# One PSUM tile for two columns, replaced after the first stage by a tile for each column

## The chip, the cores and the metric

The kernel runs on one core of a Trainium2 chip. The metric is the device time of one execution in microseconds. The median of three runs is 1278.3 us (1278.21 to 1280.56). Every duration below comes from one profiled execution.

## The reference

A channel attention is followed by two feed-forward layers, all in float32, for 6016 tokens of 256 channels.

```python
s = kn.transpose(0, 2, 1) @ qn / tau       # 256 x 256, norms over the tokens
a = softmax(s);  x = (v @ a)               # 6016 x 256
h = x @ w_in                               # 256 -> 2048
P = a0 + a1*h + a2*h**2 + a3*h**3
Q = 1 + |b0|*|h| + |b1|*h**2
y = (P / (Q + 1e-6)) @ w_out               # 2048 -> 256
gate = 1 / (1 + exp(-(y @ w_gate)))        # 256 -> 1536
val = y @ w_val
out = (gate * val) @ w_out2                # 1536 -> 256
```

## The kernel before

**Stages.** A first stage loads q and k, forms the 256 x 256 scores and the norms, and folds the attention matrix into w_in. It also converts the weights, and each float32 weight and activation becomes a high and a low part in float32r. From then on the tokens go through in 12 blocks: one of 384 tokens and eleven of 512. A block passes `moe1` (eight steps j of two 128-row slices of the 2048 hidden rows) and then `moe2` (twelve steps f of 128 rows of the 1536). `moe2` of a block is interleaved with `moe1` of the next, and the last block's `moe2` runs alone at the end, called the tail below.

**One step of `moe1`.** TensorE (PE) writes twelve matmuls of 512 columns into the two-bank tile `pH` (L796, L798, L800). ScalarE (ACT) reads `pH` three times (L808, L810, L806). VectorE (DVE) forms the fraction with L818, L812, L826, L815, L830 and L833. The last reader of `pH` is L815, called "the w product" below, and only then can the next step's matmuls write `pH`, which has one buffer. ACT rounds the result (L836), GpSimd (POOL) subtracts for the low part (L841), and PE multiplies with w_out into `pY` (L849, L851, L859).

**One step f of `moe2`.** Six matmuls form the gate column G(f) and six more the value column V(f), both 128 x 512, by the same lines L894, L896 and L898. The name of the weight (`wg` or `wv`) tells them apart. ACT takes the sigmoid of G(f) (L907, called sig(f)), DVE multiplies it with V(f) (L909, called sv(f)), ACT rounds (L912), POOL subtracts (L916), and PE multiplies with w_out2 into `pO` (L923, L931). When L870 and L872 have read `pY` of a block, the results are `yhi` and `ylo`, which G and V read.

**Where G and V lie.** PSUM has eight banks. `pH`, `pY` and `pO` take two each. The last two are the tile `gv` of shape [128, 2, 512], allocated once for the whole kernel. The class `Half` hands out `gv[:, 0, :]` for the tag `pG` and `gv[:, 1, :]` for `pV`, a bank each. The first stage and `moe1` of the first block also use both halves together (weight conversion, norms, and the temporary of four of the eight steps of the first block).

**What sets the order.** The class `Plan` holds every operation with a cost and a due time, simulates the five engines, and emits the operations in the order of the simulated starts. In its rules G(f+1) follows sig(f), V(f+1) follows sv(f), and the two columns have nothing to do with each other. The Tile framework then turns accesses to tiles into semaphore waits, in the order of emission. Each engine runs its own instructions in that order.

Of the kernel before, what the change touches and what calls it, by code (L numbers as in the profile page):

```python
# [9 lines left out]
F32 = mybir.dt.float32  # L10
# [5 lines left out]
PSUM = bass.MemoryType.PSUM  # L16
# [230 lines left out]
def c_act(n, psum, aps=0):  # L247
    return (0.052 + 0.000832 * n if psum else 0.093 + 0.000834 * n) + 0.093 * aps


def c_dve(n, aps=0):
    return 0.069 + 0.001041 * n + 0.061 * aps


def c_pool(n):
    return 0.147 + 0.002105 * n


def c_pe(n, passes=1):
    return n / 2400.0 + 0.0133 if passes == 1 else 4 * n / 2400.0 + 0.006  # L260
# [3 lines left out]
def tile_channel_attention_two_moes(  # L264
# [15 lines left out]
    P = 128  # L280
# [5 lines left out]
    NB = 512  # L286
# [20 lines left out]
    wres = ctx.enter_context(tc.tile_pool(name="wres", bufs=1))  # L307
    depth = dict(DEPTH)
    pools = {}
    gv_pool = ctx.enter_context(tc.tile_pool(name="r_gv", bufs=1, space=PSUM))  # L310
    gv = gv_pool.tile([P, 2, NB], F32, name="gv")

    class Half:

        def __init__(self, i):
            self.i = i

        def tile(self, shape, dtype, tag=None, name=None):
            return gv[:, self.i, :]

    for tag, n in depth.items():
        if tag in ("pG", "pV"):
            pools[tag] = Half("GV".index(tag[1]))
            continue
        kw = {"space": PSUM} if tag[0] == "p" else {}
        pools[tag] = ctx.enter_context(tc.tile_pool(name="r_" + tag, bufs=n, **kw))

    ident = const.tile([P, P], F32, name="ident")
    ones = const.tile([P, P], F32, name="ones")
# [547 lines left out]
    def moe2(b_, yhi, ylo):  # L877
        vp = VT if b_ else VT1
        t0, nt = blocks[b_]
        n = nt * P  # L880
        sl_ = slot[min(b_ + 1, NBLK - 1)]
        base = start[b_ + 1] + vp['base'] * sl_ / 8 + WT.get('m%d' % b_, 0.0)
        o_ps = pl.buf("pO", [P, 2, 512], at=start[b_ + 1])
        step = sl_ * NP / F2
        for f in range(F2):
            vt, d = base + f * step, sl_ / 8
            at = start[b_ + 1] + f * step
            gp = [pl.buf("pG", [P, 512], at=at), pl.buf("pV", [P, 512], at=at)]
            sg = pl.buf("sig", [P, NB], at=at)
            hi, lo = (pl.buf(t_, [P, NB], F32R, at=at) for t_ in ("hi2", "lo2"))  # L890
            for i, wt in enumerate((WG, WV)):
                def g_mm(i=i, wt=wt, gp=gp, f=f):
                    for z in range(2):
                        mm(out=gp[i].ap()[:, :n], lhsT=wt.at(f * P, 0, z), rhs=yhi.ap()[:, z, :n],  # L894
                           start=(z == 0), stop=False)
                        mm(out=gp[i].ap()[:, :n], lhsT=wt.at(f * P, 0, z), rhs=ylo.ap()[:, z, :n],  # L896
                           start=False, stop=False)
                        mm(out=gp[i].ap()[:, :n], lhsT=wt.at(f * P, 1, z), rhs=yhi.ap()[:, z, :n],  # L898
                           start=False, stop=(z == 1))
                pl.op(PE, 6 * c_pe(n), vt + (vp['G'] + i * .1) * d, g_mm, [yhi, ylo, wt.key(f * P)], [gp[i]])  # L900

            cuts = [(0, n)] if (b_, f) != (NBLK - 1, F2 - 1) else [(0, n // 2), (n // 2, n - n // 2)]
            wk = WO2.key(f * C)
            for q, (c0, m) in enumerate(cuts):
                sl = slice(c0, c0 + m)
                whole = len(cuts) == 1
                pl.op(ACT, c_act(m, 1), vt + vp['sig'] * d, lambda sg=sg, gp=gp, sl=sl: nc.scalar.activation(  # L907
                    out=sg.ap()[:, sl], in_=gp[0].ap()[:, sl], func=ACTF.Sigmoid), [gp[0]], [(sg, q)])
                pl.op(DVE, c_dve(m), vt + vp['sv'] * d, lambda sg=sg, gp=gp, sl=sl: nc.vector.tensor_tensor(  # L909
                    out=sg.ap()[:, sl], in0=sg.ap()[:, sl], in1=gp[1].ap()[:, sl], op=ALU.mult),  # L910
                    [gp[1], (sg, q)], [(sg, q)])
                pl.op(ACT, c_act(m, 0), vt + vp['hi2'] * d, lambda sg=sg, hi=hi, sl=sl: nc.scalar.activation(  # L912
                    out=hi.ap()[:, sl], in_=sg.ap()[:, sl], func=ACTF.Copy), [(sg, q)], [(hi, q)])
                e = nc.gpsimd if whole else nc.vector
                pl.op(POOL if whole else DVE, c_pool(m) if whole else c_dve(m), vt + vp['lo2'] * d,
                      lambda sg=sg, hi=hi, lo=lo, sl=sl, e=e: e.tensor_tensor(  # L916
                          out=lo.ap()[:, sl], in0=sg.ap()[:, sl], in1=hi.ap()[:, sl].bitcast(F32),
                          op=ALU.subtract), [(sg, q), (hi, q)], [(lo, q)], port=True)

                def o_hi(f=f, hi=hi, sl=sl):  # L920
                    for z in range(2):
                        for i in range(2):
                            mm(out=o_ps.ap()[:, z, sl], lhsT=WO2.at(f * C, i)[:, z * P:(z + 1) * P],  # L923
                               rhs=hi.ap()[:, sl], start=(f == 0 and i == 0), stop=False)

                pl.op(PE, 4 * c_pe(m), vt + vp['oh'] * d, o_hi, [(hi, q), wk], [(o_ps, 0), (o_ps, 1)])
            for zs in ((0, 1),) if whole else ((0,), (1,)):
                def o_lo(f=f, lo=lo, zs=zs, cuts=cuts):
                    for z in zs:
                        for q, (c0, m) in enumerate(cuts):  # L930
                            mm(out=o_ps.ap()[:, z, c0:c0 + m], lhsT=WO2.at(f * C, 0)[:, z * P:(z + 1) * P],  # L931
                               rhs=lo.ap()[:, c0:c0 + m], start=False, stop=(f == F2 - 1 and q == len(cuts) - 1))

                pl.op(PE, len(zs) * sum(c_pe(m) for _, m in cuts), vt + vp['ol'] * d, o_lo,
                      [(lo, q) for q in range(len(cuts))] + [wk], [(o_ps, z) for z in zs])
        ob = pl.buf("v", [P, 2, NB], at=start[b_ + 1] + 1.0)
        vt = base + F2 * step
        if b_ < NBLK - 1:
            pl.op(ACT, c_act(2 * n, 1), vt, lambda: nc.scalar.activation(
                out=ob.ap()[:, :, :n], in_=o_ps.ap()[:, :, :n], func=ACTF.Copy), [(o_ps, 0), (o_ps, 1)], [ob])  # L940
            pl.op(SP, max(.6, nt * .36), vt, lambda: nc.sync.dma_start(
                out=ov[:, :, t0 * P:t0 * P + n], in_=ob.ap()[:, :, :n]), [ob], (), tail=2.0)
        if b_ == NBLK - 1:
            ob2 = pl.buf("v", [P, 2, NB], at=start[b_ + 1] + 1.1)
            pl.op(DVE, c_dve(n), vt, lambda: nc.vector.tensor_copy(
                ob2.ap()[:, 1, :n], o_ps.ap()[:, 1, :n]), [(o_ps, 1)], [ob2])
            pl.op(SP, max(.6, nt * .18), vt, lambda: nc.sync.dma_start(
                out=ov[:, 1, t0 * P:t0 * P + n], in_=ob2.ap()[:, 1, :n]), [ob2], (), tail=2.0)
            pl.op(ACT, c_act(n, 1), vt, lambda: nc.scalar.activation(
                out=ob.ap()[:, 0, :n], in_=o_ps.ap()[:, 0, :n], func=ACTF.Copy), [(o_ps, 0)], [ob])  # L950
            pl.op(ACT, .6, vt, lambda: nc.scalar.dma_start(
                out=ov[:, 0, t0 * P:t0 * P + n], in_=ob.ap()[:, 0, :n]), [ob], (), tail=2.0)
# [49 lines left out]
```

## Time and profile before

| | before |
|---|---|
| median of three runs | 1278.3 us |
| profiled execution, time and span | 1278.6 us, 1276.8 us |
| PE busy | 1199.1 us (94%), 5188 matmuls |
| DVE busy | 985.8 us (77%) |
| ACT busy | 849.5 us (67%) |
| POOL busy | 513.6 us (40%) |
| chain that ended last | PE 71%, DVE 15%, ACT 7%, DMA 5%, issue 2% |

Read the table with two cautions. Matmuls are pipelined, and the modelled length of one (0.39 us) is longer than the distance between two starts. A busy PE therefore says little about time lost on it, which is read from the starts. An engine's idle time matters only where the engine that sets the end waits for it. In the timelines a bracket gives the idle time of the engine before the instruction and what ended it. "PEld" is the loading of weights, which runs one matmul ahead of PE.

### The profile page before, as it was taken

The page shows a single profiled execution, that of the slowest core. Times are in us where ns is not written, and L with a number is a line of the kernel's source. Part 1 is how long each engine was busy: PE and PEld are TensorE (multiplying, and loading weights), DVE is VectorE, ACT ScalarE, POOL GpSimd, SP SyncE. Part 2 cuts the span into 40 slices and gives each one's busy share as a digit, 9 for nine tenths or more (in the row PEclk, how much of TensorE's full clock was granted, in tenths as well). Part 3 has the DMA queues.
Part 4 walks back from the last instruction along what each step waited for, and adds up shares of the span by engine and source line. Part 5 has one row for each costly group of instructions (what it writes and reads, how often), then busy time and mean ns, then how long its engine had stood idle before and what let it go on. Part 6 is the DMA issues. An engine that isn't in the chain of part 4 may idle for free.

```text
span 1276.8 us, 13165 instructions
## 1 busy us (share of the span) xinstructions
PE 1199.1 (94%) x5188; PEld 964.0 (76%) x5188; DVE 985.8 (77%) x844; ACT 849.5 (67%) x996; POOL 513.6 (40%) x262
## 2 busy tenths in 40 slices
PE   7877799999999999999999999999999999999988
PEld 5746688777688778778778778778878878878866
DVE  3779988689789789789779789779779878878811
ACT  5798776576576677577577567567667667667522
POOL 4811245344244245245344344344344334434422
PEclk9969899999999999999999999999999999999999
DMA  9950000000100000000100100100100000000000
GB/s 362 407 206 1 17 1 1 29 1 1 34 1 1 33 1 1 34 1 1 33 1 1 34 1 1 33 1 1 33 1 1 30 5 1 17 1 1 17 1 17
DMA packets 15614, 43.32 MB, mean 34 GB/s; under 512 B 1344, under 2 KB 1856, under 8 KB 14272
## 3 DMA queue, kind: packets, MB, share of 16 engines
q1 hardware_dynamic: 15408, 42.21, 8.8%
q8 instruction: 41, 0.67, 0.2%
q10 hardware_dynamic: 144, 0.26, 0.1%
q14 instruction: 21, 0.17, 0.0%
HBM read 36.31 MB, written 6.16 MB: 33 GB/s over the span
## 4 chain that ended last, share of the span: by engine, by line
PE 71%; DVE 15%; ACT 7%; DMA 5%; issue 2%; POOL 0%; SPq 0%; ACTq 0%; DVEq 0%
PE gv L894 10%; PE gv L898 9%; PE gv L896 9%; PE pO L923 7%; PE pH L796 6%; PE pY L859 5%; PE pH L800 5%; PE pH L798 5%; PE pY L851 5%; PE pY L849 5%; PE pO L931 3%; DVE a L826 3%; ACT sig L907 3%; DVE sig L909 3%; DMA wo<-in_moe_w_out_dram 2%; DVE a L830 2%
## 5 line engine op out<-in xcount | busy, mean ns | idle before, releaser
L916 POOL TENSOR_TENSOR lo<-sig,hi 128x512 fp32r<-128x512 f32 (+1 forms) x143 | 242.7, 1703 | 416.0 <-ACT hi L912 416.0
L841 POOL TENSOR_TENSOR lo<-w,hi 128x1024 fp32r<-128x1024 f32 (+1 forms) x92 | 224.2, 2438 | 287.6 <-ACT hi L836 245.2
L830 DVE SCALAR_TENSOR_TENSOR a<-a,s 128x1024 f32<-128x1024 f32 (+1 forms) x92 | 167.7, 1822 | 55.0 <-ACT a L828 54.9
L907 ACT ACTIVATE sig<-gv 128x512 f32<-128x512 f32 (+2 forms) x145 | 84.9, 586 | 150.2 <-PE gv L898 138.7
L909 DVE TENSOR_TENSOR sig<-sig,gv 128x512 f32<-128x512 f32 (+2 forms) x145 | 97.0, 669 | 107.8 <-PE gv L898 58.4
L808 ACT ACTIVATE a<-pH,cf 128x1024 f32<-128x1024 f32 (+1 forms) x92 | 101.5, 1103 | 85.3 <-PE pH L800 84.9
L849 PE MATMUL pY<-hi,wo 128*128 128x512 f32 (+1 forms) x384 | 149.1, 388 | 5.8 <-ACT hi L836 5.8
L923 PE MATMUL pO<-hi,wo 128*128 128x512 f32 (+1 forms) x580 | 151.8, 384 | 0.4 <-ACT hi L912 0.4
L796 PE MATMUL pH<-vhi,win 128*128 128x512 f32 (+1 forms) x368 | 145.0, 394 | 5.7 <-DVE w L815 4.2
L851 PE MATMUL pY<-hi,wo 128*128 128x512 f32 (+1 forms) x384 | 148.7, 387 | 0.0
L826 DVE TENSOR_TENSOR a<-a,s 128x1024 f32<-128x1024 f32 (+1 forms) x90 | 144.2, 1602 | 4.6 <-ACT s L821 4.6
L800 PE MATMUL pH<-vhi,win 128*128 128x512 f32 (+1 forms) x368 | 143.3, 389 | 0.0
L798 PE MATMUL pH<-vlo,win 128*128 128x512 f32 (+1 forms) x368 | 143.2, 389 | 0.0
L828 ACT ACTIVATE a<-a 128x1024 f32<-128x1024 f32 (+1 forms) x96 | 100.0, 1042 | 60.1 <-DVE a L826 57.4
L833 DVE SCALAR_TENSOR_TENSOR w<-w,cf,a 128x1024 f32<-128x1024 f32 (+1 forms) x96 | 136.5, 1422 | 2.8
L894 PE MATMUL gv<-yhi,wg 128*128 128x512 f32 (+1 forms) x288 | 117.2, 407 | 21.2 <-ACT sig L907 16.4
L818 DVE SCALAR_TENSOR_TENSOR a<-a,s 128x1024 f32<-128x1024 f32 (+1 forms) x92 | 111.3, 1210 | 31.4 <-ACT s L810 29.1
L923 PEld LDWEIGHTS pO<-hi,wo 128*128 128x128 f32 x580 | 107.9, 188 | 21.6 <-ACT hi L912 0.8
L894 PE MATMUL gv<-yhi,wv 128*128 128x512 f32 (+1 forms) x288 | 112.7, 391 | 11.1 <-DVE sig L909 10.8
L836 ACT ACTIVATE hi<-w 128x1024 fp32r<-128x1024 f32 (+1 forms) x96 | 100.0, 1042 | 30.7 <-DVE w L833 30.2
L812 DVE TENSOR_TENSOR w<-w,pH 128x1024 f32<-128x1024 f32 (+1 forms) x92 | 110.8, 1204 | 8.9 <-ACT w L806 8.9
L815 DVE SCALAR_TENSOR_TENSOR w<-w,cf,pH 128x1024 f32<-128x1024 f32 (+1 forms) x92 | 116.5, 1266 | 1.5
(200 smaller groups left out, 2309.4 us busy)
## 6 DMA issues: line engine op xcount, KB each, us to landing
wo<-in_moe_w_out_dram SPq DMA_DIRECT2D x7, 1024.0 KB, 16.3
v<-in_v_dram SPq DMA_DIRECT2D x11, 512.0 KB, 3.7
out_dram<-v SPq DMA_DIRECT2D x10, 512.0 KB, 2.8
win<-in_moe_w_in_dram SPq DMA_DIRECT2D x4, 1024.0 KB, 13.7
wg<-in_kqk_dram SPq DMA_DIRECT2D x3, 1024.0 KB, 18.9
wv<-in_kqk_dram SPq DMA_DIRECT2D x3, 1024.0 KB, 15.6
win<-in_kqk_dram SPq DMA_DIRECT2D x3, 1024.0 KB, 16.6
wg<-in_moe_w_gate_dram SPq DMA_DIRECT2D x3, 1024.0 KB, 14.8
```

The lines of the kernel that those rows point to most:

```text
L796: mm(out=hp.ap()[:, i, :n], lhsT=WIN.at(f * P, 0, z), rhs=vhi.ap()[:, z, :n], start=(z == 0), stop=False)
L798: mm(out=hp.ap()[:, i, :n], lhsT=WIN.at(f * P, 0, z), rhs=vlo.ap()[:, z, :n], start=False, stop=False)
L800: mm(out=hp.ap()[:, i, :n], lhsT=WIN.at(f * P, 1, z), rhs=vhi.ap()[:, z, :n], start=False, stop=(z == 1))
L826: pl.op(POOL if t_pool else DVE, c_pool(N) if t_pool else c_dve(N), vt + vp['t'] * d, lambda: e_t.tensor_tensor(out=V(a_), in0=V(a_), in1= ...
L830: pl.op(DVE, c_dve(N), vt + vp['y'] * d, lambda: stt(out=V(a_), in0=V(a_), scalar=ATAN_C, in1=V(s_), op0=ALU.add, op1=ALU.mult), [a_] + S_ ...
L833: pl.op(DVE, c_dve(N, 1), vt + vp['g'] * d, lambda: stt(out=V(w_), in0=V(w_), scalar=col(A0), in1=V(a_), op0=ALU.add, op1=ALU.mult), [w_, ...
L841: lambda: e_lo.tensor_tensor(out=V(lo), in0=V(w_), in1=V(hi).bitcast(F32), op=ALU.subtract),
L849: mm(out=y_ps.ap()[:, z, :n], lhsT=WO.at(f * C, 0)[:, sl], rhs=hi.ap()[:, i, :n], start=(f == 0), stop=False)
L851: mm(out=y_ps.ap()[:, z, :n], lhsT=WO.at(f * C, 1)[:, sl], rhs=hi.ap()[:, i, :n], start=False, stop=False)
L894: mm(out=gp[i].ap()[:, :n], lhsT=wt.at(f * P, 0, z), rhs=yhi.ap()[:, z, :n], start=(z == 0), stop=False)
L916: lambda sg=sg, hi=hi, lo=lo, sl=sl, e=e: e.tensor_tensor(out=lo.ap()[:, sl], in0=sg.ap()[:, sl], in1=hi.ap()[:, sl].bitcast(F32), op=ALU. ...
L923: mm(out=o_ps.ap()[:, z, sl], lhsT=WO2.at(f * C, i)[:, z * P:(z + 1) * P], rhs=hi.ap()[:, sl], start=(f == 0 and i == 0), stop=False)
```

## The change

The tile `gv` is now allocated after the other pools, so that it is the last on the stack. At the first emitted gate product, `part_gv` closes the pool of `gv` and opens a pool of one bank for `pG` and another for `pV`. From there every G(f) and every V(f) gets a tile of its own from its pool, with one buffer each. Before that point both tags still mean halves of `gv`. The plan, its costs and due times, and every instruction of the five engines stay as they are.

```diff
-    gv_pool = ctx.enter_context(tc.tile_pool(name="r_gv", bufs=1, space=PSUM))
-    gv = gv_pool.tile([P, 2, NB], F32, name="gv")
-
     class Half:
-        def __init__(self, i):
-            self.i = i
+        def __init__(self, tag):
+            self.tag, self.pool = tag, None
         def tile(self, shape, dtype, tag=None, name=None):
-            return gv[:, self.i, :]
+            if self.pool is None:
+                return gv[:, "GV".index(self.tag[1]), :]
+            return self.pool.tile(shape, dtype, tag=tag, name=name)
...
-            pools[tag] = Half("GV".index(tag[1]))
+            pools[tag] = Half(tag)
...
+    both = ctx.enter_context(ExitStack())
+    gv = both.enter_context(tc.tile_pool(name="r_gv", bufs=1, space=PSUM)).tile([P, 2, NB], F32, name="gv")
+
+    def part_gv():
+        if pools["pG"].pool is None:
+            both.close()
+            for tag in ("pG", "pV"):
+                pools[tag].pool = ctx.enter_context(tc.tile_pool(name="r_" + tag, bufs=depth[tag], space=PSUM))
...
                 def g_mm(i=i, wt=wt, gp=gp, f=f):
+                    part_gv()
                     for z in range(2):
```

## Rows read from the trace of the kernel before

**Rows 1.** The page, part 1: busy time, share of span, instructions.

```profile
PE 1199.1 (94%) x5188; PEld 964.0 (76%) x5188; DVE 985.8 (77%) x844; ACT 849.5 (67%) x996; POOL 513.6 (40%) x262
```

**Rows 2.** Windows, one block: stretch, length, PE, PEld, DVE, ACT, POOL, PE clock.

```profile
729.00:826.40 97.40, 94.68 (x410) 75.98 (x409) 79.14 (x63) 65.86 (x76) 40.22 (x20) 1.00 0.04 12
```

**Rows 3.** Timeline of PE, start of that block: start, length, instruction, [idle].

```profile
731.62 0.39 PE L898 MATMUL gv<-yhi,wv 128*128 128x512 f32 x1
732.75 0.50 PE L894 MATMUL gv<-yhi,wg 128*128 128x512 f32 x1 [0.75 <-ACT sig L907]
733.09 0.40 PE L896 MATMUL gv<-ylo,wg 128*128 128x512 f32 x1
...
735.26 0.50 PE L894 MATMUL gv<-yhi,wv 128*128 128x512 f32 x1 [0.85 <-DVE sig L909]
...
737.66 0.50 PE L894 MATMUL gv<-yhi,wg 128*128 128x512 f32 x1 [0.74 <-ACT sig L907]
```

**Rows 4.** Timeline of PEld, the weight load of the matmul at 732.75.

```profile
732.75 0.19 PEld L894 LDWEIGHTS gv<-yhi,wg 128*128 128x128 f32 x1 [1.17 <-ACT sig L907]
```

**Rows 5.** Timeline of ACT, the first sigmoid of that block.

```profile
732.10 0.60 ACT L907 ACTIVATE sig<-gv 128x512 f32<-128x512 f32 x1 [0.66 <-PE gv L898]
```

**Rows 6.** Timeline, a step whose value column comes later than its sigmoid.

```profile
704.01 0.39 PE L898 MATMUL gv<-yhi,wg 128*128 128x512 f32 x1
...
704.24 0.39 PE L796 MATMUL pH<-vhi,win 128*128 128x512 f32 x1
...
704.50 0.60 ACT L907 ACTIVATE sig<-gv 128x512 f32<-128x512 f32 x1 [1.23 <-PE gv L898]
```

**Rows 7.** Waits, whole span: engine, line, releaser, total us, times, longest.

```profile
ACT sig L907 <- PE gv L898: 138.7, 125, 4.2
...
PEld gv L894 <- DVE sig L909: 32.1, 45, 1.3
...
PEld gv L894 <- ACT sig L907: 26.3, 23, 1.2
...
PE pH L796 <- DVE w L815: 4.2, 12, 2.1
```

**Rows 8.** Timeline of DVE in that block.

```profile
734.51 0.69 DVE L909 TENSOR_TENSOR sig<-sig,gv 128x512 f32<-128x512 f32 x1 [1.81 <-PE gv L898]
...
736.25 1.22 DVE L826 TENSOR_TENSOR a<-a,s 128x1024 f32<-128x1024 f32 x1
737.39 1.27 DVE L815 SCALAR_TENSOR_TENSOR w<-w,cf,pH 128x1024 f32<-128x1024 f32 x1
...
749.56 0.69 DVE L909 TENSOR_TENSOR sig<-sig,gv 128x512 f32<-128x512 f32 x1 [0.43 <-ACT sig L907]
750.17 2.33 DVE L826 TENSOR_TENSOR a<-a,s 128x1024 f32<-128x1024 f32 x1
...
758.47 1.28 DVE L815 SCALAR_TENSOR_TENSOR w<-w,cf,pH 128x1024 f32<-128x1024 f32 x1
```

**Rows 9.** Timeline of PE in that block, around two first matmuls into pH.

```profile
739.15 1.07 PE L923 MATMUL pO<-hi,wo 128*128 128x512 f32 x4
740.06 0.39 PE L796 MATMUL pH<-vhi,win 128*128 128x512 f32 x1
...
759.90 0.47 PE L796 MATMUL pH<-vhi,win 128*128 128x512 f32 x1 [0.19 <-DVE w L815]
```

**Rows 10.** Timeline of the tail, one step of the last block.

```profile
1229.66 0.50 PE L894 MATMUL gv<-yhi,wg 128*128 128x512 f32 x1
...
1233.45 0.69 DVE L909 TENSOR_TENSOR sig<-sig,gv 128x512 f32<-128x512 f32 x1 [3.84 <-ACT sig L907]
...
1234.19 0.50 PE L894 MATMUL gv<-yhi,wg 128*128 128x512 f32 x1
```

**Rows 11.** Last read of gv before the first gate product, and that product.

```profile
L830 DVE SCALAR_TENSOR_TENSOR a<-a,gv x4: 943/946/948, 109.0 to 140.7; 128x768 f32<-128x768 f32 x4
...
156.00 0.45 PE L894 MATMUL gv<-yhi,wg 128*128 128x384 f32 x1 [1.26 <-ACT yhi L870]
```

## The prediction

> **What bounds the kernel now.** I read the page's busy times first, then the windows by block, then PE's timeline in one block, and last the waits over the whole span. PE is busy 94% of the span and DVE 77% [rows 1]. In a block of 97.40 us, with the clock at its full level (1.00, that is 2.4 GHz), DVE works 79.14 us and ACT 65.86 us [rows 2]. PE's own need in a block is read from the starts. Four matmuls from 739.15 to 740.06 give 0.2275 us from start to start [rows 9], and a block has 408 of 512 columns (192 of `moe1`, 216 of `moe2`, counted in the code), so 408 x 0.227 = 92.6 us. PE thus sets the pace and loses 4.8 us in each block. The question is where.
>
> It loses most of it ahead of L894, the first matmul of a gate or value column. From 731.62 to 732.75 are 1.13 us, so 0.90 us are lost; the bracket shows 0.75 of them. By the same difference (0.15) the starts at 735.26 and 737.66 lose 1.00 and 0.89 us. Each restart costs a little more: the next matmul comes after 0.34 us (733.09) and not 0.23, which is 0.11 us [rows 3]. Over the span the weight loads ahead of L894 idle 32.1 us in 45 waits for sv and 26.3 us in 23 waits for sig [rows 7]. At 732.75 the weight load idled 1.17 us where PE lost 0.90 [rows 4, 3], so 0.27 us of each such wait is no loss: 58.4 - 68 x 0.27 = 40.0 us, and with the restarts 68 x 0.11 = 7.5 us, **47.5 us** in all.
>
> **Are these waits needed?** Three rows say that the two columns are coupled though no formula couples them.
> - sig reads the gate column alone. At 732.10 it starts 0.09 us after the end of the *value* column (731.62 + 0.39) [rows 5, 3]. Where PE turns to `pH` after the gate column, sig starts 0.10 us after the gate's own end, 704.50 against 704.01 + 0.39 [rows 6]. So sig waits for whatever was last written into `gv` ahead of it.
> - The gate column needs sig of the step before. In the tail G starts at 1234.19, 0.05 us after sv has ended (1233.45 + 0.69) [rows 10]. It waits for a reader of the other half.
> - sv reads the value column and sig's result, which were there at 732.01 and 732.70. It starts at 734.51 after 1.81 us idle, released by PE at L898 [rows 8]. That is the end of the *next* gate column, whose second matmul starts at 733.09 and whose last of four more ends near 733.09 + 4 x 0.227 + 0.39 = 734.4 [rows 3]. V at 735.26 then waits for this sv.
>
> With a tile for each column all three kinds have no ground: G(f) waits for sig(f-1), V(f) for sv(f-1), sig for G alone, sv for V alone and sig.
>
> **The change part by part.** The instructions and their order stay, so only waits move.
>
> *Waits ahead of the gate and value columns.* Removing all of them gives 47.5 us. Not all goes. At the block's start ACT is busy until 731.44 (732.10 - 0.66, rows 5). Then sig can run from 731.44 to 732.04, and G, which wants 731.85, still waits some 0.25 us and pays the 0.11 of a restart. That is 0.36 us in each of ten blocks whose `moe2` runs beside `moe1` at full width: -3.6 us. The waits at 735.26 and 737.66 go: sig and sv can finish before the columns want their banks, since ACT no longer idles 0.66 us ahead of sig and DVE no longer 1.81 us ahead of sv [rows 5, 8].
>
> *What is late next.* PE comes some 2.7 us earlier to the `pH` matmul of 740.06, which needs the w product. That ended at 737.39 + 1.27 = 738.66, 1.40 us before. Without the 1.81 us ahead of sv it ends near 736.85, and PE wants it at 737.3: enough, by 0.4 us. At 759.90 PE waits for the w product already (0.19 us idle, so 0.34 lost), and only the 0.43 us ahead of sv at 749.56 is returned there [rows 8, 9]. Such spots give and take; all the waits of `pH` for the w product sum to 4.2 us [rows 7]. Bounds: +4.2 us if the earlier DVE frees all of them, and -11 us if in each of ten blocks one DVE operation more meets a POOL operation and takes 2.33 us instead of 1.22 [rows 8]. I take 0, near the row at 759.90 where both sides gain about 0.4 us.
>
> About that clash the Trainium skill (SBUF — State Buffer, "Who interferes with whom") says that a VectorE instruction with two SBUF inputs contends with a GpSimd instruction that reads SBUF. L826 has two such inputs, and its two lengths agree. By the rule any shift of sv against POOL's subtractions can add or remove clashes, so it fixes no sign; it is the ground of the second rival.
>
> *The new tiles' own waits.* Each G and V now takes a fresh tile with one buffer, so its first matmul waits for two things: the last reader and the earlier writer. There are 144 + 144 such turns. `pH` is a tile of this kind already. At 740.06 its first matmul follows at 0.2275 us although it changes tiles [rows 9]. Lower bound 0. Upper bound one weight load that can't be taken ahead, 0.19 us [rows 4], so 288 x 0.19 = 55 us. I take 0, the value of the nearest row.
>
> *Signals.* sig needs a signal of its own at the gate column's end. At 704.01 the last gate matmul gives the signal that sig takes at 704.50, and the next matmul starts at 704.24, at the usual 0.23 us [rows 6]; cost 0. The Trainium skill (TensorE: Matmul & The Clock Gate, "The cost: per-tile semaphore tail") gives 26.3 ns for each increment when tiles of the array signal one after another. By that figure 144 more signals would be an estimated 3.8 us, and the sum below 40 us instead of 44. The row shows no trace of it.
>
> *The exchange itself.* It happens once, at the first gate product at 156.00. The last reader of the old tile ended at 140.7 + 0.95 = 141.65 [rows 11], so it hides behind 14 us of other work. The product waits there for `yhi` anyway. Cost 0, at most the few us until that wait is used up.
>
> **Sum.** 47.5 - 3.6 + 0 + 0 + 0 = 44 us. The profiled execution took 1278.6 us, of which 1.8 lie outside its span; 1278.6 - 44 = 1234.6, and the median shown is 0.3 us lower. I forecast **1234 us**. The forecast's own range is 1224 to 1245: 1278.6 - 44 - 3.6 - 4.2 - 2 of unforeseen help is about 1224, and one DVE clash more per block adds 11.
>
> **Rivals.**
> 1. *The time comes back in DVE's chain* (faster, but by about half). Near 759.90 and the other starts of `pH` the w product is the last to come, and PE that runs ahead meets it sooner. For it: DVE would have to do 79.14 us in some 93.5 us, 85%, in a fixed order, and L826 stretches from 1.22 to 2.33 us beside POOL [rows 2, 8]. Against it: DVE's idle time ahead of sv goes with the change. Price: two clashes more per block, 10 x 2 x 1.11 = 22 us, so 1257 us. It decides where the w product shifts less than PE.
> 2. *The columns stay coupled*, because the wait belongs to something else than the tile, such as the order on ACT. Then 1278 us, no change. Against it: sig after the gate column at 704.50 and after the value column at 732.10, with ACT idle before both [rows 5, 6].
> 3. *The turns of the new tiles cost PE* (slower). Place: L894, first matmul, 288 times. If every turn loses one weight load of 0.19 us, the price is 55 us against the gain of 44: 1278.6 + 11 = 1290 us. It decides from 44 / 288 = 0.15 us a turn. For it: a first matmul after a real wait does lose 0.11 us in its restart [rows 3]. Against it: 740.06, where such a turn costs nothing [rows 9].
>
> **How the numbers follow.** Forecast 0.68, first rival 0.20 (1245 to 1275), coupled 0.04, costly turns 0.06, and 0.02 for other gains below 1224. The first rival's nearer half belongs to the range, so 1224 to 1256 holds about 0.8. A measurement of this kernel can tell 0.2% (2.6 us) from no change. Faster by more than that: forecast, first rival and the last 0.02, 0.90. Within it: 0.04. Slower: 0.06.
>
> **What the changed profile would show.** Right: where the value column follows the gate column at once, sig starts about 0.1 us after the gate's last matmul, while the value column is still written. PE's waits for sv ahead of a gate column are gone, and those for sig are a small rest at the block's start. A block takes near 93.5 us instead of 97.4, and a step of the tail near 4.1 us (18 matmuls at 0.227) instead of 4.53 (1229.66 to 1234.19, rows 10). PE's count and order of matmuls are the same. Wrong: waits at L796 for the w product that grow from 4.2 us to tens; gaps ahead of L894 with no other engine to blame; sig still bound to the value column's end.

## The result, and the profile after

| | before | after |
|---|---|---|
| median, us (lowest to highest, 4 runs each) | 1278.9 (1278.21 to 1280.56) | 1221.38 (1219.74 to 1222.32) |
| profiled execution, us (its span) | 1278.6 (1276.8) | 1222.06 (1220.3) |
| ratio after/before, 95% interval | | 0.9547 [0.9531, 0.9564] |

The kernel is 57.5 us faster. I had forecast 44, and 1221.4 lies 2.6 us below the low end of my range (1224). The direction and the main mechanism were right; one term, taken as 0, was some 8 us, and the runs below say which.

The page of the changed kernel, part 1, as in [rows 1], and the first line of part 4 (the chain that ended last, by engine):

```profile
PE 1175.5 (96%) x5188; PEld 971.0 (80%) x5188; DVE 979.3 (80%) x844; ACT 846.6 (69%) x996; POOL 522.3 (43%) x262
...
PE 88%; DMA 4%; ACT 3%; DVE 3%; issue 1%; POOL 0%; SPq 0%; ACTq 0%; DVEq 0%
```

The instruction counts of PE, DVE, ACT and POOL are those of before. DVE's busy time is 6.5 us less, but that is no sign of fewer clashes with POOL, since it counts the overlap of two instructions once: the lengths of all DVE instructions add up to 1022.5 us after and 1021.0 before. Behind the first gate product 64 of the 128x1024 instructions take over 2 us, and 65 did before: ten more at L841 (L833 before), nine fewer at L834 (L826 before). PE holds 88% of the chain.

Windows of the changed kernel: the same block as in [rows 2], then a long middle stretch (columns as there).

```profile
700.10:792.96 92.86, 92.86 (x409) 76.41 (x408) 78.79 (x64) 65.82 (x76) 40.78 (x20) 1.00 0.04 12
...
400.00:900.00 500.00, 500.00 (x2198) 411.38 (x2197) 421.17 (x338) 352.05 (x408) 216.12 (x106) 1.00 0.04 13
```

The block takes 92.86 us where it took 97.40; 408 matmuls at the spacing of 0.2267 us (4.08 / 18, from the tail below) would be 92.5. The same 500 us of the kernel before:

```profile
400.00:900.00 500.00, 486.30 (x2097) 390.08 (x2096) 408.39 (x324) 338.16 (x390) 208.51 (x104) 1.00 0.03 11
```

101 more matmuls in 500 us at the same clock, 22.9 us of PE work. But the idle time to be seen before is only 13.7 us. That difference matters below: a busy share doesn't show all that PE loses.

PE at the start of the block, as in [rows 3]; the gate product at 703.85 answers to the one at 732.75:

```profile
703.48 0.39 PE L907 MATMUL pV<-yhi,wv 128*128 128x512 f32 x1
703.85 0.50 PE L903 MATMUL pG<-yhi,wg 128*128 128x512 f32 x1
704.19 0.40 PE L905 MATMUL pG<-ylo,wg 128*128 128x512 f32 x1
...
706.05 0.40 PE L903 MATMUL pV<-yhi,wv 128*128 128x512 f32 x1
706.28 0.39 PE L905 MATMUL pV<-ylo,wv 128*128 128x512 f32 x1
```

From 703.48 to 703.85 are 0.37 us, so 0.14 us are lost, and the restart takes 0.34 and not 0.23: 0.25 us in this block where I had forecast 0.36. No bracket stands beside the 0.14 us. The weight load beside it and the sigmoid that it waits for:

```profile
703.85 0.19 PEld L903 LDWEIGHTS pG<-yhi,wg 128*128 128x128 f32 x1 [0.40 <-ACT sig L916]
```

```profile
702.20 1.11 ACT L818 ACTIVATE s<-pH,cf 128x1024 f32<-128x1024 f32 x1
703.20 0.60 ACT L916 ACTIVATE sig<-pG 128x512 f32<-128x512 f32 x1
```

sig starts at 703.20, when ACT comes free, and 0.67 us before the value column is done (703.48 + 0.39). In [rows 5] it started 0.09 us behind the value column's end, after 0.66 us idle.

DVE in that block, answering to [rows 8], and the two `pH` matmuls of [rows 9]:

```profile
718.02 0.68 DVE L918 TENSOR_TENSOR sig<-sig,pV 128x512 f32<-128x512 f32 x1
718.62 2.38 DVE L834 TENSOR_TENSOR a<-a,s 128x1024 f32<-128x1024 f32 x1
...
726.98 1.28 DVE L823 SCALAR_TENSOR_TENSOR w<-w,cf,pH 128x1024 f32<-128x1024 f32 x1
```

```profile
709.03 0.39 PE L804 MATMUL pH<-vhi,win 128*128 128x512 f32 x1
...
728.53 0.39 PE L804 MATMUL pH<-vhi,win 128*128 128x512 f32 x1
```

Measured from the block's first restart (732.75 before, 703.85 after), sv moved from 16.81 to 14.17 us, the w product from 25.72 to 23.13, and the `pH` matmul from 27.15 to 24.68. So DVE gained 2.6 us, PE 2.5, and the wait of 0.34 us at this `pH` is gone. The operation that met POOL for 2.33 us still does so (2.38). One more a block now takes as long, 2.20 us at 710.39 (L841), and no `pH` matmul waits for it.

The tail, as in [rows 10], from PE's and DVE's timelines:

```profile
1185.60 0.39 PE L903 MATMUL pG<-yhi,wg 128*128 128x512 f32 x1
...
1189.68 0.39 PE L903 MATMUL pG<-yhi,wg 128*128 128x512 f32 x1
```

```profile
1188.59 0.69 DVE L918 TENSOR_TENSOR sig<-sig,pV 128x512 f32<-128x512 f32 x1 [3.39 <-PE pV L907]
```

A step takes 4.08 us instead of 4.53. The waits over the whole span, as in [rows 7]:

```profile
ACT sig L916 <- PE pG L907: 24.9, 22, 3.4
...
PEld pG L903 <- ACT sig L916: 4.0, 10, 0.4
...
PE pH L804 <- DVE w L823: 2.2, 1, 2.2
```

No weight load waits for sv any more, and sig waits for the gate column alone, 22 times instead of 125. The one long wait at `pH` (2.2 us, 2.1 before) is left; it lies ahead of the first gate product.

**The account from starts.** For each matmul after the first gate product I took the distance from the start before it, less 0.2267 us for 512 columns of that earlier matmul (less in proportion for 384 or fewer), and added these up by the tile that it writes. "First" is the first matmul behind another tile's, "later" the rest, restarts among them.

```
us beyond the spacing      before   after   returned
gate column, first          28.62    2.85      25.8
gate column, later           9.35    4.00       5.4
value column, first         13.70    0.30      13.4
value column, later          2.71    1.47       1.2
pH, first                    6.37    0.08       6.3
pH, later                    2.71    0.77       1.9
pY                           2.78    1.07       1.7
pO                           1.15    0.31       0.8
sum                         67.39   10.85      56.5
```

The first gate product itself starts at 156.00 before and 156.02 after. The span became 56.5 us shorter, so the account is complete. The gate and value columns returned 45.8 us, against 43.9 forecast. The other 10.8 us came from where I had put 0.

### The profile page after: what moved, and what is told of

The parts are those of the page before. It is cut to its first block, busy times and chain, and to the rows that moved or that the text cites. A ratio compares the mean times of both kernels' runs of the same rounds, so it can differ in the third digit from the quotient of the medians.

```text
span 1220.3 us, 13239 instructions
## 1 busy us (share of the span) xinstructions
PE 1175.5 (96%) x5188; PEld 971.0 (80%) x5188; DVE 979.3 (80%) x844; ACT 846.6 (69%) x996; POOL 522.3 (43%) x262
## 4 chain that ended last, share of the span: by engine, by line
PE 88%; DMA 4%; ACT 3%; DVE 3%; issue 1%; POOL 0%; SPq 0%; ACTq 0%; DVEq 0%
PE pO L932 10%; PE pH L804 7%; PE pH L806 7%; PE pH L808 7%; PE pY L859 6%; PE pY L857 6%; PE pY L867 6%; PE pG L903 5%; PE pG L905 5%; PE pV L903 5%; PE pV L905 5%; PE pV L907 5%; PE pG L907 5%; PE pO L940 5%; DMA wo<-in_moe_w_out_dram 3%; DMA win<-in_moe_w_in_dram 1%
## 5 line engine op out<-in xcount | busy, mean ns | idle before, releaser
L925 POOL TENSOR_TENSOR lo<-sig,hi 128x512 fp32r<-128x512 f32 (+1 forms) x143 | 248.8, 1745 | 358.1 <-ACT hi L921 358.1
L849 POOL TENSOR_TENSOR lo<-w,hi 128x1024 fp32r<-128x1024 f32 (+1 forms) x92 | 227.4, 2472 | 280.7 <-ACT hi L844 226.9
L826 DVE SCALAR_TENSOR_TENSOR a<-a,s 128x1024 f32<-128x1024 f32 (+1 forms) x92 | 111.3, 1210 | 44.8 <-ACT s L818 42.0
L841 DVE SCALAR_TENSOR_TENSOR w<-w,cf,a 128x1024 f32<-128x1024 f32 (+1 forms) x96 | 144.8, 1509 | 2.8
L918 DVE TENSOR_TENSOR sig<-sig,pV 128x512 f32<-128x512 f32 (+2 forms) x145 | 96.6, 667 | 54.2 <-PE pV L907 53.3
L834 DVE TENSOR_TENSOR a<-a,s 128x1024 f32<-128x1024 f32 (+1 forms) x90 | 138.1, 1534 | 0.0
L921 ACT ACTIVATE hi<-sig 128x512 fp32r<-128x512 f32 (+2 forms) x145 | 90.3, 623 | 54.7 <-DVE sig L918 54.4
L844 ACT ACTIVATE hi<-w 128x1024 fp32r<-128x1024 f32 (+1 forms) x96 | 100.5, 1047 | 25.1 <-DVE w L841 22.7
L903 PE MATMUL pG<-yhi,wg 128*128 128x512 f32 (+1 forms) x288 | 112.3, 390 | 2.4 <-ACT yhi L878 2.4
L916 ACT ACTIVATE sig<-pG 128x512 f32<-128x512 f32 (+2 forms) x145 | 85.4, 589 | 39.6 <-PE pG L907 24.9
L905 PE MATMUL pG<-ylo,wg 128*128 128x512 f32 (+1 forms) x288 | 111.4, 387 | 1.3 <-DVE ylo L880 1.3
```

Of the source, the lines that this page charges most:

```text
L841: pl.op(DVE, c_dve(N, 1), vt + vp['g'] * d, lambda: stt(out=V(w_), in0=V(w_), scalar=col(A0), in1=V(a_), op0=ALU.add, op1=ALU.mult), [w_, ...
L849: lambda: e_lo.tensor_tensor(out=V(lo), in0=V(w_), in1=V(hi).bitcast(F32), op=ALU.subtract),
L925: lambda sg=sg, hi=hi, lo=lo, sl=sl, e=e: e.tensor_tensor(out=lo.ap()[:, sl], in0=sg.ap()[:, sl], in1=hi.ap()[:, sl].bitcast(F32), op=ALU. ...
```

## The experiments

Two questions were open. Is the whole gain the orders that the shared tile had brought, or is some of it another effect of the two tiles? And why did `pH`, whose inputs the change doesn't touch, return 8.2 us?

All kernels but one keep the two tiles of the changed kernel and put back, by an explicit dependency, orders that the one tile had brought. `tie` makes an instruction wait for the one last issued of the named kind. The edit, shortened, is the same in all, and only `KEEP` differs:

```diff
+    KEEP = (("sig", "V"),)
+    emitted = {}
+    def tie(i, kind, *after):
+        for x in after:
+            if (kind, x) in KEEP and x in emitted:
+                tc.add_manual_dep(i.ins, emitted[x].ins.name, ...)
+        return i
...
+                        if z == 0:
+                            tie(k, "GV"[i], ("sv", "sig")[i])
...
+                    emitted["GV"[i]] = k
...
-                 ... nc.scalar.activation(... Sigmoid) ...
+                 ... emitted.update(sig=tie(nc.scalar.activation(... Sigmoid), "sig", "V", "sv")) ...
```

sv is tied in the same way. The pair ("sig", "V") reads: sig waits for the end of the value column last issued. The kernel before ran beside them on the same chips: 1278.59 us for the first four, 1279.16 for the others. Losses below are against the changed kernel's 1221.38, which ran in another series, beside a kernel before of 1278.9. "The changed kernel's" losses by starts are those of the table above.

**All five orders put back.**

```diff
+    KEEP = (("sig", "V"), ("G", "sv"), ("sv", "G"), ("V", "sig"), ("sig", "sv"))
```

> Two tiles as in the changed kernel, but with the five orders of the one tile put back by hand as explicit dependencies: sig after the last value column, a gate column after the last sv, sv after the last gate column, a value column after the last sig, sig after the last sv. Theory (the gain is these waits and nothing else): the time of the kernel before, 1276 to 1281 us, with the waits ahead of L894's lines back at some 58 us. Rival (part of the gain comes from the banks that moved, or from the tiles' own turns): clearly below, 1265 us or less.

Measured: 1277.99 us, ratio to the kernel before 0.9994 [0.9985, 1.0003]. The waits, whole span (columns as in [rows 7]):

```profile
ACT sig L929 <- PE pV L919: 113.4, 94, 4.2
...
PEld pG L913 <- ACT sig L929: 25.6, 22, 1.2
...
PEld pV L913 <- DVE sig L931: 16.2, 13, 1.3
...
PEld pG L913 <- DVE sig L931: 15.4, 31, 0.7
...
PE pH L814 <- DVE w L833: 4.1, 12, 2.1
```

sv's two rows together are 31.6 us in 44 waits, against 32.1 in 45 in [rows 7]. The account from starts agrees too: gate column 28.46 + 9.27, value column 13.41 + 2.63, `pH` 6.32 + 2.85. The two tiles with the old orders are the old kernel, so the orders are the whole gain, `pH`'s part included.

**Two one-bank tiles that are allocated once**, so that no G or V takes a fresh tile.

```diff
-            return self.pool.tile(shape, dtype, tag=tag, name=name)
+            return self.one
...
+                pools[tag].one = pools[tag].pool.tile([P, NB], F32, tag=tag, name=tag)
```

> Two one-bank tiles as in the changed kernel, but each allocated once and written again and again, so that there are no turns of fresh tiles. Theory (a turn costs PE nothing): 1221 us, within 2 us, with the same starts. Rival (each of the 288 turns costs something that the gain of the change hides): faster, by 288 times the price of a turn; 0.02 us a turn would be 6 us, 1215 us.

Measured: 1220.71 us (1220.02 to 1220.82), ratio 0.9543 [0.9529, 0.9558]; the changed kernel has 0.9547 [0.9531, 0.9564]. The 288 turns of the tiles cost nothing that can be measured.

**sig waits for the value column again**, everything else free.

```diff
+    KEEP = (("sig", "V"),)
```

> The changed kernel with one order put back: sig waits for the last value column written. Theory A (this order holds up ACT, through it DVE's w product, and so also pH): the waits ahead of the second and third gate column of a block come back, 10 x 2 x 1.0 = 20 us, and the 8 us ahead of pH too: 1249 us. Theory B (pH was late because DVE's queue stood at sv): the 20 us alone, 1241 us, with pH's waits as small as in the changed kernel.

Measured: 1252.95 us, ratio 0.9799 [0.9783, 0.9816]; 31.6 us of the gain are lost, and of the two figures the 1249 is the near one. PE's timeline and the waits:

```profile
720.32 0.50 PE L913 MATMUL pG<-yhi,wg 128*128 128x512 f32 x1 [0.75 <-ACT sig L929]
...
724.08 0.50 PE L913 MATMUL pG<-yhi,wg 128*128 128x512 f32 x1 [0.74 <-ACT sig L929]
...
746.36 0.47 PE L814 MATMUL pH<-vhi,win 128*128 128x512 f32 x1 [0.19 <-DVE w L833]
```

```profile
ACT sig L929 <- PE pV L919: 100.2, 104, 4.2
...
PE pH L814 <- DVE w L833: 4.4, 13, 2.1
```

The gate column's first matmuls lose 21.25 us (18.4 more than in the changed kernel) and `pH` 9.4, all that it lost before, in 22 waits of 0.24 to 0.43 us. `pH` itself is untouched by this edit. The chain of work that ended last shows the way from sig to the `pH` matmul at 746.36 (start, length, engine and line):

```profile
735.39 0.60 ACT sig L929
736.02 0.69 DVE sig L931
...
744.93 1.29 DVE w L833
```

Sig has waited for the end of a value column (0.84 us of idle time on ACT). A late sig makes a late sv, sv stands ahead of the w product in DVE's order, and `pH` waits for the w product. Between sig and `pH` the chain holds work of DVE and ACT alone.

**sv waits for the gate column issued last.**

```diff
+    KEEP = (("sv", "G"),)
```

> The changed kernel with one order put back: sv waits for the last gate column written. Theory A: the wait ahead of the second value column of a block comes back, 10 x 1.1 us, and two such waits in the first block, 2 us: 1234 us, without pH's 8 us. Theory B (the time lost ahead of pH is this order's): 1242 us, with some 8 us lost ahead of pH by PE's starts.

Measured: 1243.36 us, ratio 0.9726 [0.9712, 0.9741]: the 1242, not the 1234. PE's timeline of one block shows both places:

```profile
717.01 0.50 PE L913 MATMUL pV<-yhi,wv 128*128 128x512 f32 x1 [0.85 <-DVE sig L931]
...
721.45 0.47 PE L814 MATMUL pH<-vhi,win 128*128 128x512 f32 x1 [0.47 <-DVE w L833]
```

The value column loses 13.13 + 3.07 us again, and `pH` 6.20 + 1.86, now in ten waits of 0.6 us where before it was 21 of 0.24 to 0.36. These are not the old waits. They stand 4.4 us behind the restart of the value column, and ahead of each of the ten L844 (L826 before) takes 2.06 to 2.10 us, beside a subtraction on POOL:

```profile
717.73 1.30 POOL L938 TENSOR_TENSOR lo<-sig,hi 128x512 fp32r<-128x512 f32 x1 [10.26 <-ACT hi L934]
```

```profile
718.01 2.10 DVE L844 TENSOR_TENSOR a<-a,s 128x1024 f32<-128x1024 f32 x1
```

At 1.22 us, which the same operation takes in the changed kernel (at 706.22), the w product would have ended near 720.4, before PE wanted `pH` at 720.8. So the 1242 came about, but by a way that neither theory had named: the late sv and this clash together. The kernel with sig alone set free, below, has the late sv without the clash.

**The gate column waits for sv.**

```diff
+    KEEP = (("G", "sv"),)
```

> The changed kernel with one order put back: a gate column waits for the last sv. Theory A (this order costs only because sig was late): sv now ends before most gate columns start, by 0.40 us in the tail, and only three starts a block are some 0.1 to 0.25 us too early for it, so 10 x 0.6 = 6 us, 1227 us, and nothing in the tail. Rival (this order is the cause of the tail's wait of 0.27 us a step, whatever sig does): a step of the tail 4.5 us, 5 us more, 1232 us.

Measured: 1230.44 us, ratio 0.9621 [0.9607, 0.9636]; 9.1 us lost where 6 were expected. The gate column loses 14.5 us instead of 6.85, `pH` 0.8 as in the changed kernel. The tail's step stays at 4.08 us:

```profile
1182.01 0.39 PE L913 MATMUL pG<-yhi,wg 128*128 128x512 f32 x1
...
1186.09 0.39 PE L913 MATMUL pG<-yhi,wg 128*128 128x512 f32 x1
```

The changed kernel's own wait at the block's start (0.14 us) stays. Beyond it this order costs PE two starts in each block, 32 and 72 us later (in one block 0.20 us at 740.47 and 0.25 at 780.33, each with 0.11 for the restart). In the tail an early sig lets sv end before G is due.

**Both of the two main orders.**

```diff
+    KEEP = (("sig", "V"), ("sv", "G"))
```

> The changed kernel with two orders put back: sig after the value column and sv after the gate column. Theory A (either of the two makes the w product late, so the loss ahead of pH comes back once, not twice): 1221 + 31 + 14 = 1266 us. Rival (the two add up): 1221 + 31 + 22 = 1274 us.

Measured: 1267.72 us, ratio 0.9906 [0.989, 0.9923]: the 1266, not the 1274. `pH` loses 9.6 us, and the gate column (21.28 + 6.07) and the value column (13.21 + 2.51) about what each order alone brings. The figure was right, the reason only in part. `pH`'s 22 waits are those of the kernel where sig alone is held back, behind the value column (0.24 to 0.43 us). The ten waits of 0.6 us of the kernel where sv alone is held back, behind the gate column, don't arise: L844 takes 1.22 us in that place in all ten blocks (at 732.34 in one). So it is not one loss that either order brings, but two, and the second is absent when sig is held back too.

**sig alone set free**, all other orders back.

```diff
+    KEEP = (("G", "sv"), ("sv", "G"), ("V", "sig"), ("sig", "sv"))
```

> The kernel before (all five orders by hand) with one taken away: sig no longer waits for the value column. Theory A: the gate columns' 18 us go and the tail's step falls to 4.1 us, but the value column's 13 us and pH's 8 us stay, since sv still waits for the gate column: 1248 us. Rival (sig is the one lever, and sv only follows it): the value column's and pH's waits shrink too, 1235 us or less.

Measured: 1243.29 us, ratio 0.972 [0.9706, 0.9735]; between the two figures (1235 and 1248). My account of it was wrong: I had `pH`'s loss stay, and it is gone (0.57 us).

```profile
PEld pV L913 <- DVE sig L931: 16.2, 13, 1.3
...
ACT sig L929 <- DVE sig L931: 13.7, 20, 0.8
...
PEld pG L913 <- DVE sig L931: 9.9, 21, 0.7
...
PE pH L814 <- DVE w L833: 2.1, 1, 2.1
```

sv is just as late here as in the kernel with sv alone held back: in all ten blocks of both, DVE idles 1.04 to 1.07 us ahead of it. But L844 takes 1.22 us in all ten:

```profile
717.96 1.22 DVE L844 TENSOR_TENSOR a<-a,s 128x1024 f32<-128x1024 f32 x1
```

POOL's subtraction starts only at 718.48 here, since sig (717.28) has waited for sv. A late sv without the clash thus costs `pH` nothing.

The value column loses 16.6 us and the gate column 14.1, 7.2 more than in the changed kernel. These 7.2 belong to the order of the gate column behind sv, which is kept here: they stand at the same two starts of a block (747.31 and 787.07) as in the kernel with that order alone, where they were 7.6. That this kernel and the one with sv alone held back take the same time (1243.29 and 1243.36) is two different losses of one size, 7.2 us at the gate column here and 7.2 at `pH` there.

**sv alone set free**, all other orders back.

```diff
+    KEEP = (("sig", "V"), ("G", "sv"), ("V", "sig"), ("sig", "sv"))
```

> The kernel before (all five orders by hand) with one taken away: sv no longer waits for the gate column. Theory A: the value column's 13 us go, the gate columns' and the tail's waits and pH's 8 us stay, since sig still waits for the value column: 1264 us. Rival (sv is the lever): pH's loss goes as well, 1256 us or less.

Measured: 1263.23 us, ratio 0.9877 [0.9863, 0.9892]: the 1264, not the 1256. The value column's loss is gone (1.27 us left), the gate column's (28.57 + 9.08) and `pH`'s (9.3) stay.

Set free alone, sig returns 35.9 us and sv 15.9 (against the 1279.16 beside them), of the 57.5 that all five return. Put back alone, the two main orders cost 31.6 and 22.0, and put back together 46.3. The 7.2 us between are what `pH` loses more than in the changed kernel when sv alone is held back.

So the second question is answered by sig: `pH` loses 9.1 to 9.6 us in each of the five kernels where sig waits for the value column, and 0.6 to 0.9 in each where it doesn't, but for the one with the clash (8.1).

## Why the prediction missed its range

**Right.** *The bound and the reason.* PE sets the pace, the columns were coupled by the tile alone, and with the orders back the time is back at 1277.99. The second rival (coupled by something else) falls with sig at 703.20 and the first experiment. *The turns of the new tiles, 0*: the third rival's 55 us would show between 1221.38 and 1220.71, and don't. *Signals, 0*: 18 matmuls of a tail step take 4.08 us, that is 0.2267 each, with the signals in them; the trace shows nothing of the 3.8 us that I had worked out by the Trainium skill's section "The cost: per-tile semaphore tail" (TensorE: Matmul & The Clock Gate). *The signatures*: block 92.86 (forecast 93.5), tail step 4.08 (4.1), waits for sv gone, a small rest for sig.

**Nearly right, by two errors that cancel.** Ahead of L894 I had 47.5 us lost, and it was 54.4; I had 3.6 stay, and 8.6 stay. The return was 45.8 for 43.9. Taking 0.27 us off each weight load's wait gave 40.0 us ahead of the columns, where it was 42.3. Behind them I had 7.5 for the restarts, and it was 12.1: two waits for `ylo` (0.82 and 1.03 us) and some 1370 delays of less than 0.02 us, 2.5 together, stood in no term. Of the 8.6 left, 6.85 are at the gate column: the rest for sig at the blocks' starts, the wait for `yhi` and `ylo` ahead of the tail, and a stretch at the lower clock (last section).

**Wrong: the step "What is late next", which took 0 with +4.2 us as its upper end.** `pH` returned 8.2 us. Two faults are in the step.

*The bound was no bound.* I took 4.2 us from the waits of `pH` for the w product [rows 7] as all there was to get. By starts, `pH` lost 9.1 us after the first gate product. Half of the 4.2 was one wait of 2.1 us ahead of the first gate product, which is still there. The other 2.1 us stand for 21 waits: ten of 0.24 us and eleven of 0.32 to 0.36, 6.37 us with all smaller ones, and there are 2.71 more in the restarts and the rest behind them. A row counts only idle time beyond the modelled end of a matmul (0.39 us after its start, against a spacing of 0.2267), so each wait is short by 0.16 us. The eleven make up the 2.1 us; the ten of 0.24 leave 0.08 of idle time each and don't stand in the row. I had used this very difference ahead of L894 (0.15 us on each bracket) and at 759.90 (0.34 lost for 0.19 shown), and left it out of the bound.

*The sign was taken for open, and it was not.* At 759.90 I let DVE return only the 0.43 us of idle time ahead of that sv, and PE arrive 0.4 us earlier, so that both sides cancelled. But the chain ahead of that `pH` matmul starts at PE itself. The last matmul of a value column, before and after:

```profile
748.45 0.39 PE L898 MATMUL gv<-yhi,wv 128*128 128x512 f32 x1
```

```profile
717.42 0.39 PE L907 MATMUL pV<-yhi,wv 128*128 128x512 f32 x1
```

In the kernel before sig waits for its end (748.84), and the chain of work that ended last goes from there to the `pH` matmul at 759.90:

```profile
748.93 0.61 ACT sig L907
749.56 0.69 DVE sig L909
...
758.47 1.29 DVE w L815
```

The value column's last matmul came 2.13 us earlier behind the block's first restart (15.70 before, 13.57 after), and DVE's chain came earlier with it. The 0.43 us came on top: sv moved by 2.64 us, the w product by 2.59 and `pH` by 2.47. From that matmul to `pH` are 11.45 us before and 11.11 after, less by just the 0.34 us of the wait. So an earlier PE uses nothing up of what DVE gives back, and the waits of `pH` were no new limit that the gain would meet, but part of the same loss: a late sig makes a late sv, and sv is in front of the w product. Putting sig's order back alone brings 8.6 us back at `pH`, and setting sig alone free takes them away (0.57 us left). The first rival, that the time comes back in DVE's chain, is not borne out here. Its clash did come, once more a block at L841 (and once less at L834), but no `pH` matmul waited for it; in the kernel with sv alone held back such a clash, at L844, cost the 7.2 us at `pH`.

`pY` and `pO` returned another 2.5 us, of small delays inside their groups. `pY`'s 1.7 follow the order of sig: 2.7 to 2.8 in each kernel where sig waits for the value column, 1.07 to 1.09 in each where it doesn't. What makes them was not tried.

So 43.9 was right to 1.9, and 10.8 us of `pH`, `pY` and `pO` stood outside it. With the bound read from starts (+9.1, and +2.5 for the small delays) the range would have reached to 1278.6 - 44 - 3.6 - 11.6 - 2, about 1217.

## What to carry to other kernels

Two halves of one on-chip tile that have readers and writers of their own are ordered as one here: look for an operation that starts just behind the end of a half that it doesn't read, and price every order that this makes, also through the engine's queue behind the held operation. Take PE's losses from start to start over all matmuls of a kind. The idle times in PE's own rows were too small here (0.19 us for 0.34 lost), those of the weight load too large (1.17 for 0.90), and a bound on what can be won needs the loss itself. Before taking two shifts as cancelling, ask whether the engine that is awaited was itself waiting for the one that now comes earlier. When an order that is put back brings a loss of the expected size, look where the waits stand: they can be others.

## What the runs showed of the chip that I had not expected

At the start of the tail PE waits for `yhi` and `ylo` in both kernels alike, 1.11 and 0.76 us. After it the changed kernel's PE runs for a short time at the lower clock. PE's timeline:

```profile
1163.78 0.49 PE L903 MATMUL pG<-yhi,wg 128*128 128x512 f32 x1 [1.11 <-ACT yhi L878]
1165.04 0.50 PE L905 MATMUL pG<-ylo,wg 128*128 128x512 f32 x1 [0.76 <-DVE ylo L880]
...
1166.79 0.63 PE L903 MATMUL pV<-yhi,wv 128*128 128x512 f32 x1
1167.22 0.63 PE L905 MATMUL pV<-ylo,wv 128*128 128x512 f32 x1
...
1169.25 0.39 PE L903 MATMUL pG<-yhi,wg 128*128 128x512 f32 x1
```

The windows, 20 us around this place after, and then before:

```profile
1160.00:1180.00 20.00, 18.12 (x72) 14.29 (x71) 3.29 (x4) 5.31 (x8) 4.91 (x4) 0.91 0.00 1
```

```profile
1200.00:1220.00 20.00, 17.38 (x74) 13.39 (x73) 9.31 (x7) 7.67 (x9) 6.89 (x4) 1.00 0.07 26
```

Some seven matmuls start 0.43 us apart, the spacing at 1.2 GHz, and not 0.2267: about 1.4 us. In the kernel before, the granted clock stays at 1.00 after the same two waits. In the 13 us ahead of them PE waited for nothing in either. The kernel with its two tiles allocated once, whose order is the same as the changed kernel's, also stays at 1.00 from 1160 to 1180 us, so the change alone doesn't decide it. What does stays open.
